# Fewer identity filler products in the attention of the first batch, with a new order table

## The chip, the core and the metric

The kernel runs on one core of a Trainium2 chip. The metric is the device time of one execution in microseconds (us); lower is better. Engines are called as in the profile: PE (TensorE, matrix products; PEld is its weight loading), DVE (VectorE), ACT (ScalarE), POOL (GpSimd) and SP (SyncE, which issues nearly all DMAs). A line L259 stands for every instruction of the first part of the program, because one helper issues them all; instructions are told apart by the names of their tiles.

## The reference

A gated linear attention, a token and channel mixer, and a gated MLP, over 4 batches of 768 positions, 8 heads of 48 channels:

```python
f = 1.0 / (1.0 + np.exp(-f_logit))
for t in range(S):
    state = f[:, :, t, :, None] * state + np.einsum('bhd,bhe->bhde', k[:, :, t], v[:, :, t])
    y[:, :, t] = np.einsum('bhd,bhde->bhe', q[:, :, t], state)
...
theta = x @ w_theta
zr, zi = x * np.cos(theta), x * np.sin(theta)
y = np.einsum('ts,bsd->btd', w_tok_r, zr) + np.einsum('ts,bsd->btd', w_tok_i, zi)
u = x + y
u + np.maximum(u @ w_ch, 0.0)
...
h = np.maximum(x @ w_in, 0.0)
u, v = (h[..., :d_ff // 2], h[..., d_ff // 2:])
v_s = np.einsum('ts,bsd->btd', w_spatial, layer_norm(v)) + b_spatial[None, :, None]
(u * v_s) @ w_out
```

(`layer_norm(v)` stands for four lines that subtract the mean and divide by the standard deviation.)

## The kernel before

**Attention of the first batch.** The positions are cut into chunks of 64, so that the recurrence becomes products. Heads go in pairs, called units u; each batch has four of them, and for the first batch each unit is done in two halves h of 384 positions (`half_att`). A half of a unit is a chain over the engines. DVE turns the gates into decays (`icp`, `cw`) and scales k and q with them (`k`, `q`). PE transposes k (`pt`, `half_k`), forms the masked scores (`psc`, `att_s`, then `sc` on DVE) and the outer products of k and v (`pw`, `half_w`); ACT copies those to `cu`, DVE scans over the chunks in `cu`, and PE multiplies q with the scanned states and the scores with v into the two output banks `px` (`half_x`). ACT copies the banks into the batch's activations `X`.

**Filler products.** Right after `half_x` takes its two output banks, it calls `warm`, which multiplies the 128x128 identity with itself four times into the first of them; the results are overwritten by the real products. In the trace they read `px<-ident`. Each fp32 product has two records, so four of them are 8 records. At the very start 16 more identity products are put into a bank `pt` (`FILL`); those stay.

**Mixer of the first batch.** `xt` are transposes of X, `pth` is theta, ACT and DVE make cosine and sine (`sn`) and multiply by X (`z`). The token weights come in 12 blocks by DMA into one of two buffers `ws` as 64-bit numbers and are turned into floats by one ACT step and three DVE steps (`tk<-ws`); the weights of theta (`ft`) and of the channel product (`wb`, `wc`) take the same way through `ws`. PE sums `acc<-tk,z`, 36 products for the first 384 output positions, then `hh` is the channel product. Batches 1 to 3 follow with split operands (three products each) while their own attention is still being computed. From 352.6 us of the span on the MLP of all batches runs (`pv`, `pu`, `pg`, `po`).

**What sets the order.** `Plan` records every instruction and its dependences; a table `LINE`, with one list of unit numbers for each queue (T for PE, V for DVE, A for ACT, G for POOL, Q for SP), gives the order in which each engine issues its units in everything before the MLP. A unit is one instruction, or on PE a group of products between two calls of `group`. An engine works strictly through its list, so an instruction that waits holds up all that stand behind it.

Of the kernel before, what the change touches and what calls it, by code (L numbers as in the profile page):

```python
# [80 lines left out]
    ],  # L81
# [18 lines left out]
    ],  # L100
# [19 lines left out]
    ],  # L120
# [1247 lines left out]
```

## Time and profile before

| | us |
|---|---|
| timed runs, median of 3 | 595.83 (594.65 to 596.77) |
| the profiled execution's own time | 598.03 |
| span of that execution | 596.3 |
| PE busy | 581.0 (97%) |
| DVE busy | 452.0 (76%) |
| ACT busy | 352.8 (59%) |
| mean granted PE clock | 0.997 |

The span runs from the first to the last instruction of the profiled execution; its own time is 1.7 us longer. Shares are means over the whole span; the attention of the first batch fills about its first 55 us.

### The profile page before, as it was taken

What the parts mean: (1) busy time and instruction counts of PE and PEld (TensorE: products, weight loads), DVE (VectorE), ACT (ScalarE), POOL (GpSimd) and SP (SyncE); (2) the same over time, 40 slices, a digit from 0 to 9 for tenths busy, and PEclk for the clock granted to TensorE, in tenths of its full rate; (3) what the DMA queues carried; (4) which work ended last, traced back from release to release, by engine and by line L of the source; (5) the groups of instructions that cost most, each with busy time, mean ns of one, the idle gap of its engine ahead of it and who ended that gap; (6) DMA issues with size and microseconds to landing.
All of it is one profiled execution on the core that took longest, in us unless ns stands there. A gap on an engine that the chain in (4) does not pass through costs nothing.

```text
span 596.3 us, 14184 instructions
## 1 busy us (share of the span) xinstructions
PE 581.0 (97%) x5750; PEld 533.3 (89%) x5750; DVE 452.0 (76%) x816; ACT 352.8 (59%) x683; POOL 29.1 (5%) x95
## 2 busy tenths in 40 slices
PE   7899998999999999999999999999999999999995
PEld 6776676877999999999999989999999999999995
DVE  6898998899887777764868587983968396839681
ACT  7798896598877888754664146623642364246421
POOL 5320110000000000000000000000000000000000
PEclk9999999999999999999999999999999999999998
DMA  7779966686978887778789999896049604940422
GB/s 240 209 240 333 281 200 250 226 287 210 304 240 307 271 311 247 256 249 282 244 282 320 338 354 299 288 373 212 1 139 373 203 1 147 371 145 0 158 89 78
DMA packets 68585, 139.44 MB, mean 234 GB/s; under 512 B 6496, under 2 KB 40800, under 8 KB 68512
## 3 DMA queue, kind: packets, MB, share of 16 engines
q1 hardware_dynamic: 68368, 138.36, 68.9%
q8 instruction: 47, 0.77, 0.6%
q14 instruction: 26, 0.21, 0.1%
q10 hardware_dynamic: 144, 0.10, 0.1%
HBM read 104.20 MB, written 31.85 MB: 228 GB/s over the span
## 4 chain that ended last, share of the span: by engine, by line
PE 91%; DMA 3%; DVE 2%; issue 1%; ACT 1%; SPq 1%; POOL 0%; DVEq 0%; ACTq 0%; POOLq 0%
PE acc L259 27%; PE pg L259 15%; PE po L259 9%; PE pu L259 8%; PE pv L259 8%; PE hh L259 6%; PE pth L259 6%; PE px L259 3%; PE psc L259 3%; PE pw L259 2%; PE pt L259 2%; DMA ws<-tok_dram 1%; SPq L259 1%; DMA k<-kd_dram 1%; DVE icp L259 1%
## 5 line engine op out<-in xcount | busy, mean ns | idle before, releaser
L259 PE MATMUL acc<-tk,z 128*128 128x384 f32 x792 | 172.4, 369 | 0.0
L259 PEld LDWEIGHTS acc<-tk,z 128*128 128x128 f32 x792 | 138.3, 189 | 15.8
L259 PE MATMUL pg<-sp,vn 128*128 128x384 f32 x504 | 88.0, 336 | 0.0
L259 PEld LDWEIGHTS pg<-sp,vn 128*128 128x128 f32 x504 | 87.4, 188 | 0.0
L259 PE MATMUL po<-wo,gt 128*128 128x384 f32 x288 | 51.3, 338 | 0.0
L259 PEld LDWEIGHTS po<-wo,gt 128*128 128x128 f32 x288 | 50.8, 188 | 0.0
L259 PE MATMUL pu<-x,wi 128*128 128x384 f32 x288 | 50.7, 335 | 0.0
L259 PEld LDWEIGHTS pu<-x,wi 128*128 128x128 f32 x288 | 50.1, 188 | 0.3
L259 PE MATMUL pv<-wi,x 128*128 128x512 f32 x216 | 49.8, 390 | 0.0
L259 PEld LDWEIGHTS pv<-wi,x 128*128 128x128 f32 x216 | 40.5, 188 | 8.2
L259 PE MATMUL hh<-uT,wc 128*128 128x384 f32 x216 | 41.9, 341 | 0.6 <-DVE uT L259 0.4
L259 ACT ACTIVATE gt<-g 128x384 fp32r<-128x384 f32 x32 | 16.7, 523 | 43.1 <-DVE g L259 42.5
L259 PEld LDWEIGHTS hh<-uT,wc 128*128 128x128 f32 x216 | 37.7, 188 | 1.6 <-DVE uT L259 0.9
L259 DVE TENSOR_TENSOR vn<-vr,vn 128x768 fp32r<-128x768 f32 x24 | 22.9, 955 | 16.1 <-ACT vn L259 15.8
L259 ACT ACTIVATE vn<-vr 128x768 fp32r<-128x768 f32 x24 | 20.2, 844 | 20.4 <-PE pg L259 17.9
L259 PE MATMUL pth<-wh,xT 128*128 128x384 f32 x108 | 31.9, 350 | 0.0
L259 DVE BATCH_NORM_STATS2 st<-vr 128x6 f32<-128x512 f32 x24 | 16.1, 687 | 19.6 <-ACT vr L259 19.6
L259 PE MATMUL px<-vc,sc 64*64 64x48 f32 x768 | 27.1, 220 | 0.2
L259 ACT ACTIVATE ws<-ws 128x768 f32<-128x768 f32 (+2 forms) x28 | 20.7, 738 | 10.4 <-DMA ws<-wo_dram 4.2
L259 ACT ACTIVATE oo<-po 128x384 f32<-128x384 f32 (+1 forms) x24 | 11.6, 482 | 24.8 <-PE po L259 23.7
L259 ACT ACTIVATE sn<-sn 128x384 f32<-128x384 f32 x48 | 24.3, 520 | 2.9 <-DVE sn L259 2.7
L259 PEld LDWEIGHTS px<-vc,sc 64*64 64x64 f32 x768 | 24.7, 140 | 0.5 <-DMA vc<-va_dram 0.3
(141 smaller groups left out, 1055.0 us busy)
## 6 DMA issues: line engine op xcount, KB each, us to landing
sp<-wpd SPq DMA_DIRECT2D x56, 576.0 KB, 5.9
tk<-tkp SPq DMA_DIRECT2D x48, 384.0 KB, 5.0
ws<-tok_dram SPq DMA_DIRECT2D x12, 768.0 KB, 5.9
tkp<-tk SPq DMA_DIRECT2D x24, 384.0 KB, 5.0
tkd<-tk SPq DMA_DIRECT2D x12, 384.0 KB, 5.7
x2d<-xt SPq DMA_DIRECT2D x24, 192.0 KB, 4.5
ws<-tkd SPq DMA_DIRECT2D x12, 384.0 KB, 4.9
xs<-x2d SPq DMA_DIRECT2D x12, 384.0 KB, 3.9
```

What stands on the lines that cost most here:

```text
L259: r = f(*a, **k)
```

## The change

`half_x` calls `warm` in the first halves alone, so that of 32 filler products in the `px` banks 16 are left. With four units fewer on PE the numbers of later units fall, and the table `LINE` is replaced by another one, which also orders the remaining units differently on all five queues. The rest of the program is the same.

```diff
@@ half_x
         ps = [self.bank("px") for _ in range(2)]
-        self.warm(ps[0])
+        if h == 0:
+            self.warm(ps[0])
         self.group()
@@ LINE, list "T"
-        45, 46, 47, 48, 49, 50, 51, 52, 53, 61, 54, 55, 56, 57, 82, 58, 59, 60, 95, 100, 91, 101, 121, 128, 132, 137, 144, 138, 148, 153, 154, 159,
...
+        45, 46, 47, 48, 61, 49, 50, 51, 52, 53, 54, 55, 82, 56, 57, 58, 59, 60, 95, 100, 91, 101, 121, 128, 132, 137, 144, 138, 148, 153, 154, 163,
...
```

How the table moves instructions is shown at three places. The first is the start of PE's queue, where identity products stand among the transposes of the first two k tiles. Before:

```order
L259 MATMUL pt<-ident 128x128 x9
L259 MATMUL pt<-ident,k_137 128x128 x3
L259 MATMUL pt<-ident 128x128 x4
L259 MATMUL pt<-ident,k_203 128x128 x3
L259 MATMUL pt<-ident 128x128 x3
L259 MATMUL pw<-vn_100,kt 64x48 x12
```

Now:

```order
L259 MATMUL pt<-ident 128x128 x4
L259 MATMUL pt<-ident,k_137 128x128 x3
L259 MATMUL pt<-ident 128x128 x7
L259 MATMUL pt<-ident,k_203 128x128 x3
L259 MATMUL pt<-ident 128x128 x5
L259 MATMUL pw<-vn_100,kt 64x48 x12
```

Of the 16 identity products five have moved from ahead of the first transposes to behind them.

The second place is PE's queue in the first half of the last unit (u = 3), where the `pw` products feed the scan that the last `px` row waits for:

```order
+L259 MATMUL pw<-vn_101,kt 64x48 x12
 L259 MATMUL psc<-qp_107,kp 64x64 x12
-L259 MATMUL pw<-vn_101,kt 64x48 x12
 L259 MATMUL px<-ident 128x128 x4
 L259 MATMUL px<-cu_480,qp_107 64x48 x2
```

The `pw` products now stand ahead of the scores; the fillers of this first half are still there.

The third place is DVE's queue in the second halves, around the first token block (`tk0_1011` before, `tk0_995` now) and the scan of unit 1 (`cu11`). Before:

```order
L259 TENSOR_SCALAR tk0_1011<-ws_1012 128x768
L259 SCALAR_TENSOR_TENSOR tk0_1011<-ws_1012,tk0_1011 128x768
L259 TENSOR_TENSOR k3_938<-k3_938,icp_98 128x768
L259 SCALAR_TENSOR_TENSOR tk0_1011<-ws_1012,tk0_1011 128x768
L259 TENSOR_TENSOR sc0_108<-psc_748,mask_91 128x384
```

Now:

```order
L259 TENSOR_SCALAR tk0_995<-ws_996 128x768
L259 SCALAR_TENSOR_TENSOR cu11_688<-cu11_688 128x336
L259 SCALAR_TENSOR_TENSOR tk0_995<-ws_996,tk0_995 128x768 x2
L259 TENSOR_TENSOR k3_922<-k3_922,icp_98 128x768
L259 TENSOR_TENSOR sc0_108<-psc_740,mask_91 128x384
```

The step on k of the next batch's first group (`k3`) used to stand between the last two steps on the block and now stands behind both, so the `ws` buffer is read out one step sooner.

## Rows read from the trace of the kernel before

**Rows 1.** The page: busy time of the engines, and granted PE clock in 40 slices.
```profile
PE 581.0 (97%) x5750; PEld 533.3 (89%) x5750; DVE 452.0 (76%) x816; ACT 352.8 (59%) x683; POOL 29.1 (5%) x95
...
PEclk9999999999999999999999999999999999999998
```

**Rows 2.** Stretches: start:end, length, busy PE, PEld, DVE, ACT, POOL (records), clock, DMA share, GB/s.
```profile
0.00:54.60 54.60, 48.09 (x908) 39.42 (x908) 46.34 (x80) 43.76 (x103) 17.49 (x60) 1.00 0.78 250
54.60:110.00 55.40, 53.60 (x881) 38.23 (x882) 50.96 (x72) 45.04 (x84) 5.81 (x12) 1.00 0.76 253
110.00:200.00 90.00, 89.80 (x1132) 78.41 (x1131) 75.98 (x105) 71.62 (x123) 2.44 (x15) 1.00 0.79 262
...
300.00:352.60 52.60, 52.18 (x298) 51.61 (x297) 39.39 (x68) 22.26 (x41) 0.10 (x1) 1.00 0.96 339
```

**Rows 3.** Timeline of PE, fillers of the second halves: start, length, what, [idle before <-releaser].
```profile
29.80 1.06 PE L259 MATMUL px<-ident 128*128 128x128 f32 x8
30.71 2.20 PE L259 MATMUL pth<-ft,xt 128*128 128x384 f32 x6
...
38.48 1.05 PE L259 MATMUL px<-ident 128*128 128x128 f32 x8
...
43.63 1.05 PE L259 MATMUL px<-ident 128*128 128x128 f32 x8
44.90 0.39 PE L259 MATMUL px<-cu,qp 64*64 64x48 f32 x8 [0.21 <-DVE cu L259]
...
50.07 1.05 PE L259 MATMUL px<-ident 128*128 128x128 f32 x8
```

**Rows 4.** Waits from 0 to 60 us: who <- for whom, total, times, longest.
```profile
PE px L259 <- DVE cu L259: 2.4, 4, 1.2
```

**Rows 5.** Timeline of DVE, 20 to 54 us.
```profile
20.42 0.86 DVE L259 TENSOR_TENSOR_SCAN cu<-cu 128x336 f32<-128x336 f32 x1 [0.37 <-ACT cu L259]
...
24.93 0.86 DVE L259 TENSOR_TENSOR_SCAN cu<-cu 128x336 f32<-128x336 f32 x1 [0.52 <-ACT cu L259]
...
29.74 0.36 DVE L259 TENSOR_SCALAR ft<-ws 128x384 uint32<-128x384 uint32 x1 [0.31 <-ACT ws L259]
30.13 1.15 DVE L259 SCALAR_TENSOR_TENSOR ft<-ws,ft 128x384 uint32<-128x384 uint32 x2
31.63 0.56 DVE L259 TENSOR_TENSOR k<-k,icp 128x384 f32<-128x384 f32 x1 [0.35 <-DMA k<-kd_dram]
...
41.32 0.96 DVE L259 SCALAR_TENSOR_TENSOR tk<-ws,tk 128x768 uint32<-128x768 uint32 x1
...
51.11 0.56 DVE L259 TENSOR_SCALAR tk<-ws 128x768 uint32<-128x768 uint32 x1 [1.26 <-ACT ws L259]
...
53.57 0.95 DVE L259 TENSOR_TENSOR z<-sn,X 128x768 f32<-128x768 f32 x1
```

**Rows 6.** Timelines of SP and ACT: the third token block's issue and its first step.
```profile
43.09 1.46 SPq L259 DMA_DIRECT2D ws<-tok_dram  x1
...
50.17 0.90 ACT L259 ACTIVATE ws<-ws 128x768 f32<-128x768 f32 x1 [1.76 <-DMA ws<-tok_dram]
```

**Rows 7.** Timelines of DVE, ACT and PE, 79 to 89 us.
```profile
79.31 0.53 DVE L259 TENSOR_TENSOR wc<-wb,wc 128x384 fp32r<-128x384 f32 x1
...
86.81 0.94 ACT L259 ACTIVATE qp<-q,live 128x768 f32<-128x768 f32 x1 [0.84 <-DVE q L259]
...
87.81 0.92 PE L259 MATMUL psc<-qp,k 64*64 64x64 f32 x24
```

**Rows 8.** Timeline of PE, the longest wait after 60 us.
```profile
98.75 1.71 PE L259 MATMUL psc<-qp,kp 64*64 64x64 f32 x47 [1.56 <-issue]
```

**Rows 9.** Timeline of PE, the first products.
```profile
2.33 3.88 PE L259 MATMUL pt<-ident 128*128 128x128 f32 x18 [2.33 <-POOL ident masks.py:199]
6.35 0.55 PE L259 MATMUL pt<-ident,k 128*128 128x128 f32 x3
6.73 1.06 PE L259 MATMUL pt<-ident 128*128 128x128 f32 x8
```

124 rows, old and new, of the table LINE are left out of this document.

## The prediction, made before the changed kernel ran

> **What bounds the kernel now.** I read the page first. PE is busy for 581.0 of 596.3 us and its clock stands at full in 39 of 40 slices [rows 1], which makes PE look like the bound everywhere. The table of stretches corrects that [rows 2]. From 110 us to the MLP, PE has next to no idle time (0.20 us of 90, then 0.42 us of the 52.6 before the MLP), so every microsecond that PE is ahead at 110 us comes off the end. But in the first 54.6 us PE is busy for only 48.09, and part of that is filler; DVE is busy there for 46.34 us. The five waits of DVE that I find from 20 us on sum to 2.8 of the 8.3 us that are left [rows 5]; most of the others lie at the start, before the first loads are there. The waits between the engines confirm the direction: PE waits for the scans of DVE, four times, 2.4 us in all [rows 4]. So until about 90 us the question for every PE step is whether DVE has its input ready, and what counts is how fast DVE gets through its list, not how much PE has to do.
>
> **The fillers.** The four groups that go take 1.06, 1.05, 1.05 and 1.05 us of PE time [rows 3]. From the start of one to the start of what follows it was 0.91 us for the first (30.71 less 29.80) and about 1.0 for the rest: 3.9 us in all. The third group shows what this is worth by itself: behind it PE still waited 0.21 us for the scan, so without the group it would wait 1.2 us and gain nothing. Nor did any filler of a second half hold DVE up: the DVE waits that I find after 29.80 us are one for a loaded k, one for a token block [rows 5] and none for PE. **Taken alone I cost the removal at 0**, covered by DVE's list; the ends are 0 and -3.9. What it does is to make PE able to follow if DVE gets faster.
>
> **DVE's list.** Up to the step that makes the third z block (at 53.57 us before [rows 5]) the new table puts the same DVE instructions ahead, in another order. So DVE can reach it sooner only by losing waits. One by one:
> - 0.52 us before the scan of unit 3's first half. Its `pw` products, which ACT has to copy first, now stand ahead of the scores, whose 24 records take 0.92 us in the like row [rows 7]; that is more than the wait. Gone: -0.52.
> - 0.37 us before the scan of unit 2's first half. In the new list the steps on the f and cw of later units stand ahead of it, so DVE arrives later than its copies: -0.37. The same steps then no longer stand behind it, so nothing is added.
> - 0.35 us for the second half of k of unit 2, and 0.31 us for the third block of theta weights. Both loads are issued sooner: in SP's list the k load goes from place 39 to 34, ahead of the first token block (768 KB) and no longer behind the gates of the next batch, and the weight load goes from 35 to 23. -0.66.
> - 1.26 us for the third token block. Its load could be issued only when DVE had read out the buffer of the first block, which ended at 41.32 + 0.96 = 42.28; the issue came at 43.09 and ACT could begin only at 50.17 [rows 5, 6]. The step on k3 (0.95 us) now stands behind that read-out instead of inside it, so of DVE's work 0.95 us more lies between release and need. The wait shrinks by that, to 0.3: -0.95.
>
> Together -2.5 us. Against it stands the start. Of the 16 identity products there, nine ran before the first transposes, at 3.88 / 9 = 0.43 us each; the next four took 1.06 us, 0.265 each [rows 9]. That ratio is what two clock levels, 1.2 and 2.4 GHz, would make, and the rise comes after the first nine, although the profile's clock column says full from the beginning. Now four run first, PE then waits for k until about 6.35, and 12 instead of 7 stand between there and `pw`. If PE is fast from there on, `pw` is 5 x 0.265 = 1.3 us later than before; if all 12 run at the slow pace, 5.2 instead of 1.9, so 3.3 us later. DVE meanwhile has the three steps of the first theta block to do, which the new list puts ahead of the first scan: 0.36 + 1.15 = 1.5 us by the same steps later on [rows 5]. What DVE then waits is between 0 and 1.8 us. I take 0.6, because the rise should come part of the way through the 12, as it came within the first 4 us before. So DVE reaches the third z block 2.5 - 0.6 = 1.9 us sooner.
>
> **From 55 to 110 us.** The tightest place is the scores of unit 6: qp is ready at 86.81 + 0.94 = 87.75 and PE starts at 87.81 [rows 7], so PE was on time within 0.06 us. Ahead of the q that feeds it the new list has the same DVE steps but one, a subtraction for the channel weights (0.53 us [rows 7]), which has moved behind: -0.53. PE has done the same 28 token products by then in both orders, and has 3.9 us of filler less, so it can follow a shift of 1.9 + 0.53 = 2.4 us. What it does with the rest is wait. Afterwards there is one long wait, 1.56 us before the scores of unit 7, for which the profile names no releaser [rows 8]. I cannot say what makes it, so I leave it as it is, at 0; the bounds are its loss and a second one like it, -1.56 and +1.56.
>
> **From 110 us on** the same products run in another order, with waits of 0.6 us before the MLP at most to win. I cost this at 0; it holds as long as PE's inputs are not later than PE, which its almost unbroken busy time speaks for. The MLP's order is the same.
>
> **Sum:** -2.5 + 0.6 - 0.53 = **-2.4 us**. The profiled execution took 598.03 us with a span of 596.3, so it would take 595.6 with a span of 593.9. The timed runs lie lower, at 595.83, and I set the forecast against them: **593.4 us**. A difference under 0.3%, 1.8 us, is about what a measurement of this kernel cannot tell from none.
>
> **Rivals.**
> - *DVE keeps its waits.* A list without one wait often gains another, and the loads are close: DMA is 0.78 busy in the first stretch [rows 2], and the first token block now waits at SP for a buffer with loads of v and k behind it. If the gains on DVE's list come back as waits for those, only the 0.53 is left: 595.3 us. For it speaks that three of the five gains hang on transfers; against it that the wait for the third block shrinks whatever the DMAs do, as long as SP issues on time.
> - *All of it arrives.* The start costs nothing, the whole 1.26 us goes, and the unexplained wait goes too: -(0.37 + 0.52 + 0.66 + 1.26 + 0.53 + 1.56) = -4.9, so 590.9 us. PE's 3.9 us and its own waits of 2.4 us [rows 4] would allow it. Against it: five things must go right.
> - *The clock falls.* This one ends slower. The fillers kept PE working while it waited for scans; without them a second half holds a wait of some 1 us at each of four places. If PE then ran the next 3.9 us at the slow pace, as it did over its first nine products [rows 9], each place would cost 3.9 x (1 - 0.265 / 0.43) = 1.5 us, 6.0 for four, against the 3.9 that PE is freed of: +2.1 us, and the gain of DVE is lost because PE comes too late for it: 597.9 us. With two falls or fewer PE still arrives before DVE and the forecast stands. The trace speaks against it: the clock stayed at 1.00 through the wait of 1.56 us [rows 2, 8], and PE keeps more work around these places than it had in the first halves.
>
> The Trainium skill speaks for the last rival (TensorE: Matmul & The Clock Gate, section "HAM oscillation — how this bites in real kernels"): a PE that idles between bursts of products is put back to half clock and begins the next burst cold. By that rule, if it bit at all four places, the time would be the 597.9 us above; by the trace, where waits of that size left the clock at full, it is 593.4.
>
> **How the numbers follow.** I give the forecast 0.50, DVE keeping its waits 0.24, all of it arriving 0.11, and the clock with whatever else the new order spoils 0.15. The forecast's own range is 592.0 to 595.2: the start between 0 and 1.8 us, and one of the two transfer gains lost. Faster by over 1.8 us means under 594.0; of the forecast's 0.50 I count 0.40 there and 0.10 above. With the second rival that is 0.51 faster. Same: 0.10 + 0.22 from the first rival + 0.02 from the last = 0.34. Slower: 0.02 from the first rival, where the unexplained wait doubles, and 0.13 from the last, 0.15. The range that holds it 8 times in 10 reaches from the second rival to the last: 590.9 to 597.9 us.
>
> **What would show it.** Right: the third z block on DVE starts near 51.7 instead of 53.57, DVE's wait before the third token block is under 0.5 us, the scans of units 2 and 3 wait for nothing, the scores of unit 6 start near 85.4, and PE's waits in the first 54.6 us add up to more than before with the span shorter nevertheless. The start is wrong if DVE waits over 1 us for the first `cu` or `psc`. The forecast as a whole is wrong if the third z block does not come sooner, if a clock below 1.00 or filler-sized products slower than 0.3 us appear between 25 and 55 us, or if PE has new waits after 110 us of over 1 us.

## The result and the profile after

The change makes the kernel slower: median 600.63 us of 6 runs (598.98 to 603.06) against 596.30 of 6 runs beside it (594.65 to 597.05), a ratio of 1.0081, 95% interval [1.0055, 1.0107]. The prediction of 593.4 (590.9 to 597.9) was wrong in sign. The profiled execution took 600.52 us with a span of 598.7, 2.4 more than before. The profiled execution of the kernel before took 598.03 us, more than any of the six runs beside the change, so the two traces side by side show 2.4 of the 4.3 us between the medians.

The page, and the table of stretches with the columns of [rows 2]:

```profile
PE 579.4 (97%) x5718; PEld 532.1 (89%) x5718; DVE 450.2 (75%) x816; ACT 353.0 (59%) x683; POOL 32.3 (5%) x95
```
```profile
0.00:54.60 54.60, 45.70 (x872) 37.79 (x873) 45.42 (x80) 43.34 (x102) 19.03 (x61) 0.97 0.77 247
54.60:110.00 55.40, 52.62 (x878) 36.74 (x877) 49.22 (x70) 45.95 (x85) 4.94 (x11) 1.00 0.76 240
110.00:200.00 90.00, 90.00 (x1135) 79.12 (x1135) 77.25 (x106) 68.78 (x122) 5.13 (x17) 1.00 0.77 266
```

Against [rows 2], PE has 32 records fewer to do, but DVE, which sets the pace, does less in each of the first two stretches (45.42 and 49.22 us instead of 46.34 and 50.96). From 110 us PE is saturated as before. And the clock of the first stretch is no longer 1.00.

**The start.** Timeline of PE, the rows that answer to [rows 9], and then the waits of DVE at the start:

```profile
1.60 2.07 PE L259 MATMUL pt<-ident 128*128 128x128 f32 x8 [1.60 <-POOL ident masks.py:199]
6.54 0.90 PE L259 MATMUL pt<-ident,k 128*128 128x128 f32 x3 [2.86 <-DVE k L259]
7.24 3.20 PE L259 MATMUL pt<-ident 128*128 128x128 f32 x14
10.22 0.85 PE L259 MATMUL pt<-ident,k 128*128 128x128 f32 x3
12.28 0.56 PE L259 MATMUL pw<-vn,kt 64*64 64x48 f32 x24
```
```profile
7.08 0.19 DVE L259 RECIPROCAL fs<-f 128x6 f32<-128x6 f32 x1 [0.60 <-ACT f L259]
7.83 0.36 DVE L259 TENSOR_SCALAR ft<-ws 128x384 uint32<-128x384 uint32 x1 [0.55 <-ACT ws L259]
14.90 0.56 DVE L259 TENSOR_TENSOR sc<-psc,mask 128x384 f32<-128x384 f32 x1 [0.36 <-PE psc L259]
```

PE waits 2.86 us for k, and the seven products behind it take 3.20 / 7 = 0.46 us each: still the slow pace. `pw` comes at 12.28 instead of 8.96 us in the timeline of the kernel before, 3.3 later. DVE waits for f1, the theta weights and the scores, 1.5 us in all.

**20 to 54 us.** Timeline of DVE, rows that answer to [rows 5]:

```profile
23.05 0.86 DVE L259 TENSOR_TENSOR_SCAN cu<-cu 128x336 f32<-128x336 f32 x1
...
27.97 0.86 DVE L259 TENSOR_TENSOR_SCAN cu<-cu 128x336 f32<-128x336 f32 x1 [1.09 <-POOL ge L259]
...
30.26 0.56 DVE L259 TENSOR_TENSOR icp<-cw,icp 128x384 f32<-128x384 f32 x1 [0.52 <-ACT ws L259]
...
35.73 0.86 DVE L259 TENSOR_TENSOR_SCAN cu<-cu 128x336 f32<-128x336 f32 x1 [0.86 <-ACT cu L259]
...
51.86 0.55 DVE L259 TENSOR_SCALAR tk<-ws 128x768 uint32<-128x768 uint32 x1
52.45 1.95 DVE L259 SCALAR_TENSOR_TENSOR tk<-ws,tk 128x768 uint32<-128x768 uint32 x2
54.32 0.95 DVE L259 TENSOR_TENSOR z<-sn,X 128x768 f32<-128x768 f32 x1
```

The waits for the scan of unit 2, for k, for the weights and for the third token block are gone, as forecast. Three others have come. The third z block starts at 54.32 instead of 53.57. Behind the 1.09 us stands ACT, in its timeline:

```profile
24.44 1.72 ACT L259 ACTIVATE f<-f 128x768 f32<-128x768 f32 x2 [1.43 <-DMA f<-fd_dram]
26.07 0.45 ACT L259 ACTIVATE X<-px 128x144 f32<-128x144 f32 x2
26.41 0.44 ACT L259 ACTIVATE cu<-kp 128x288 f32<-128x288 f32 x1
```

ACT now works on the gates f3 of the next batch ahead of the copies of units 2 and 3, and waits there for a load; the copies that PE and the scan need stand behind. (The profile puts DVE's wait down to POOL, the last of its semaphores.) The 0.86 us has SP behind it: the first token block was issued ahead of v, so PE's `pw` of the second half waits for v.

```profile
26.39 0.81 PE L259 MATMUL pw<-vn,kt 64*64 64x48 f32 x19 [0.87 <-ACT X L259]
...
27.95 1.74 PE L259 MATMUL px<-ident 128*128 128x128 f32 x8
...
34.50 0.56 PE L259 MATMUL pw<-vn,kt 64*64 64x48 f32 x24 [0.74 <-DMA vn<-vu_dram]
```

After the first of these two waits the granted clock fell to 0.50, that is 1.2 GHz, though the fillers of the first halves are all there: the four at 27.95 take 1.74 / 4 = 0.44 us each. From 32 us on the clock is 1.00 again, and it stays there after the second wait. One row per us, columns as in [rows 2]:

```profile
27.00:28.00 1.00, 1.00 (x35) 0.93 (x31) 0.03 (x1) 0.62 (x3) 0.13 (x1) 1.00 0.80 202
28.00:29.00 1.00, 1.00 (x7) 1.00 (x7) 1.00 (x2) 0.97 (x3) 0.11 (x1) 0.68 1.03 249
29.00:30.00 1.00, 1.00 (x19) 0.78 (x18) 0.74 (x2) 1.00 (x3) 0.37 (x2) 0.50 0.67 160
30.00:31.00 1.00, 1.00 (x40) 0.98 (x36) 0.70 (x2) 0.52 (x2) 0.00 (x0) 0.50 0.92 301
```

**55 to 110 us.** The waits of PE, which answer to [rows 7, 8]:

```profile
89.27 1.61 PE L259 MATMUL psc<-qp,k 64*64 64x64 f32 x48 [0.59 <-ACT qp L259]
...
97.51 1.65 PE L259 MATMUL pw<-vn,kt 64*64 64x48 f32 x46 [2.19 <-ACT X L259]
99.09 2.85 PE L259 MATMUL acc<-tk,z 128*128 128x384 f32 x8
```

The wait of 1.56 us before the scores of unit 7 is gone, but the `pw` ahead of them now wait 2.19 us.

### The profile page after: what moved, and what is told of

It reads as the page before. It is cut to its first block, busy times and chain, and to the rows that moved or that the text cites. A ratio compares the mean times of both kernels' runs of the same rounds, so it can differ in the third digit from the quotient of the medians.

```text
span 598.7 us, 14114 instructions
## 1 busy us (share of the span) xinstructions
PE 579.4 (97%) x5718; PEld 532.1 (89%) x5718; DVE 450.2 (75%) x816; ACT 353.0 (59%) x683; POOL 32.3 (5%) x95
## 4 chain that ended last, share of the span: by engine, by line
PE 89%; DMA 4%; DVE 3%; issue 1%; ACT 1%; SPq 1%; POOL 0%; DVEq 0%; ACTq 0%
PE acc L259 25%; PE pg L259 15%; PE po L259 8%; PE pu L259 8%; PE pv L259 8%; PE hh L259 6%; PE pth L259 6%; PE px L259 3%; PE pt L259 3%; PE psc L259 3%; PE pw L259 2%; DMA f<-fd_dram 1%; DMA vn<-vu_dram 1%; DMA ws<-wc_dram 1%; DMA ws<-tok_dram 1%
```

## The experiments

Each run stands beside runs of the kernel before that were made with it. The ratio is not the quotient of the two medians.

| run | median | before beside it | ratio, 95% interval |
|---|---|---|---|
| fillers alone | 595.76 | 596.84 | 0.9990 [0.9975, 1.0005] |
| order alone | 609.36 | 596.84 | 1.0206 [1.0168, 1.0244] |
| no px fillers | 598.56 | 597.08 | 1.0033 [1.0020, 1.0045] |
| order of before to 54 us | 599.15 | 596.74 | 1.0045 [1.0027, 1.0063] |
| changed order to 54 us | 598.33 | 596.74 | 1.0031 [1.0005, 1.0058] |
| changed order to 20 us | 598.30 | 597.08 | 1.0035 [1.0015, 1.0054] |

**Fillers alone and order alone.** The units of the four groups (228, 265, 281, 296) are taken out of PE's list and the others renumbered; or they are put back into the list of the change.

```diff
-            self.warm(ps[0])
+            if h == 0:
+                self.warm(ps[0])
...
-        300, 302, 228, 304, 229,
+        296, 298, 300, 228,
```

> The order of before, with the four filler groups of the second halves left out and nothing moved. Before: 596.3 us; the change: 600.6. The start theory (the change loses because PE's identity products at the start were moved behind the first transposes, so that `pw` comes 3.3 us later) expects no difference from before: 595.5 to 597, and `pw` at 9.0 us of the span as before. The clock theory (without fillers PE is put back to half clock) expects half-clock stretches between 30 and 52 us and 598 to 600. The order theory (the rest of the table loses) expects 595 to 597.

> The table of the change with the four filler groups put back at the places they had before. The start theory expects a time at or above that of the change, 600 to 604, since the 3.3 us lost at the start stay and PE has 3.9 us more to do. The clock theory expects 596 to 598. The order theory expects 600 to 603.

Without the fillers and with nothing moved, 0.9990: no loss. The order with the fillers loses 2.06%. So the order loses, and the fillers hide nothing of it: in the new order they cost 1.0206 less 1.0081, 1.25% or 7.5 us, more than their 3.9 us of PE. In that profile the clock of 54.6 to 110 us is 0.94, in that of the change 1.00, and PE has waits of 1.02, 1.45 and 1.52 us between 185 and 270 us, where the change has one of 0.75.

**Early or late.** Two hybrids without the fillers: every list follows one order as far as it was by 54 us, then takes what is left in the other. The first hybrid begins with the order of before, the second with the changed one. In PE's list of the first, for instance:

```diff
@@ LINE, list "T"
-        293, 409, 431, 446, 458, 340, 342, 386, 432, 344,
+        293, 431, 386, 340, 342, 409, 446, 458, 432, 344,
```

> The second-half fillers left out; every queue in the order of before as far as it was by 54 us, from there the changed order for all that is left. The run with the fillers left out of the order of before took 595.76 us (596.84 for the kernel before beside it), the change 600.6. Early theory (the changed table loses in the first 54 us, where DVE, ACT and SP wait in new places, and only carries that loss on): 595 to 597. Late theory (it loses after 54 us, by a wait like that of 2.19 us for ACT's X at 97.5 us, and by the clock): 599 to 601. If both halves carry part: about 598.

> The complement: the changed order as far as each queue was by 54 us in the changed kernel, from there the order of before, second-half fillers left out. Early theory: 599 to 601. Late theory: 595.5 to 597. Both: about 598.

Both lose. Against the fillers alone, the late part costs 1.0045 less 0.9990, 3.3 us, the early part 2.4 us; together 5.7 us. The change stands 1.0081 less 0.9990, 5.4 us, above the fillers alone, so the two parts make up its loss, within the intervals.

**The late part.** In the first hybrid PE's wait is the only one over 0.2 us from 52 to 110 us, and what follows is at half clock:

```profile
94.43 1.68 PE L256 MATMUL pw<-vn,kt 64*64 64x48 f32 x46 [2.33 <-ACT X L256]
96.04 5.33 PE L256 MATMUL acc<-tk,z 128*128 128x384 f32 x8
```
```profile
92.00:94.00 2.00, 0.10 (x1) 0.00 (x0) 0.52 (x2) 0.80 (x2) 0.11 (x1) 1.00 0.98 240
94.00:96.00 2.00, 1.57 (x46) 1.52 (x46) 1.82 (x3) 1.09 (x4) 0.00 (x0) 0.56 1.01 377
96.00:98.00 2.00, 2.00 (x6) 1.17 (x4) 1.33 (x3) 1.78 (x5) 0.00 (x0) 0.50 0.58 220
```

ACT's list in that trace, where the copies X that the `pw` need stand behind a step on a token block:

```profile
93.20 0.88 ACT L256 ACTIVATE ws<-ws 128x768 f32<-128x768 f32 x1 [2.19 <-DMA ws<-tok_dram]
93.98 0.69 ACT L256 ACTIVATE X<-px 128x288 f32<-128x288 f32 x2
```

The same edit on the change and on this hybrid puts two groups of token products (545 and 558) ahead of the `pw` of unit 7 (563). The kernel before has one of the two there, 545; the change had moved it behind.

```diff
@@ LINE, list "T"
-        557, 554, 559, 563, 545, 558, 568,
+        557, 554, 559, 545, 558, 563, 568,
```

> The change with one edit on PE: ahead of the `pw` products of unit 7, which wait 2.19 us for ACT's copies X at 97.5 us, go the two groups of token products (`acc`, 1.4 us each) that the change put behind them; before had one of them there. If that wait and the half-speed stretch that can follow it are the late loss, the wait shrinks to 0 to 0.3 us and the time falls by 2 to 3.5 us, to 597 to 598.5. If the waits only move on, 600 to 601.

> The same edit on the hybrid with the order of before up to 54 us (599.15), whose PE waited 2.33 us at 94.4 and then ran at half clock for 6.8 us. If this one place is the whole late loss: 595.5 to 597, and no half clock between 90 and 105 us. If the later order loses elsewhere too: 598 to 599.

Measured: 598.89 against 596.37, 1.0040 [1.0022, 1.0059], and 596.37 against 596.37, 0.9990 [0.9971, 1.0008]: 2.4 us less in the change (1.0081 less 1.0040), 3.3 us less in the hybrid. In the hybrid the eight records of `acc` take 2.85 us instead of 5.33, and of the wait 0.27 us is left:

```profile
92.72 2.85 PE L256 MATMUL acc<-tk,z 128*128 128x384 f32 x8
95.50 1.65 PE L256 MATMUL pw<-vn,kt 64*64 64x48 f32 x48
...
98.24 0.91 PE L256 MATMUL psc<-qp,kp 64*64 64x64 f32 x23 [0.27 <-issue]
```

That one place is the whole late loss, 1.0045 to 0.9990, though the edit puts one group more ahead of the `pw` than the kernel before has there. PE had nothing left to do while ACT's copies X, behind a step that waits 2.19 us for a token block (2.11 in the change), were late.

In the order of before the same copies stand behind the same step. Whether they make its wait of 1.56 us [rows 8]:

```diff
@@ LINE, list "A"
-        562, 517, 527, 560, 561, 506,
+        562, 517, 560, 561, 527, 506,
```

> The order of before without the second-half fillers (595.76), with one edit on ACT: the two copies X of unit 6, which stand behind a step on a token block that waits 1.7 us for its load, go ahead of that step. If the wait of 0.6 to 1.6 us before the scores of unit 7, for which the profile names no releaser, comes from these late copies, it goes, and the time falls to 594.5 to 595.5. If it has another cause, 595.5 to 596.5 and the wait stays.

595.65 against 596.37, 0.9993 [0.9974, 1.0013], and the wait stays:

```profile
97.53 0.73 PE L256 MATMUL psc<-qp,kp 64*64 64x64 f32 x17 [1.50 <-issue]
```

So they don't; what does is open.

**The early part, its middle.** Three edits on the waits between 20 and 35 us: the gate steps f3 on ACT back (on the change), the load of the first token block on SP back (on the second hybrid), and both with ACT's step on that block (on the second hybrid).

```diff
@@ LINE, list "A"
-        149, 150, 326, 327, 155, 156,
+        149, 150, 155, 156,
...
+        297, 299, 326, 327, 241,
@@ LINE, list "Q"
-        195, 367, 216, 253, 191, 233, 217, 252, 192,
+        195, 216, 253, 191, 233, 217, 252, 367, 192,
```

> The change with one pair of ACT's steps moved: those on the gates f3 of the next batch, which ACT reaches at 23 us and then waits 1.43 us for their load, go back behind the copies `xt`, where before had them; nothing else. If that wait makes the late X and the late scan of unit 3 (DVE waits 1.09 us for it) and sets the lag after, the third z block comes about 1.0 to 1.5 us sooner than in the change (54.3) and the time falls by 1 to 1.5, to 599.2 to 599.7. If the lag is set elsewhere (start, loads of v, the later order), 600 to 601.

> The hybrid with the changed order up to 54 us (598.33), with one edit on SP: the load of the first token block (768 KB, 1.5 us to issue), which the change put ahead of the loads of v for the second halves, goes behind them. If that load makes PE wait 1.59 us for vn at 33.5 and DVE 1.22 us for the scan behind it, both waits fall under 0.4 us, the third z block comes 0.8 to 1.3 us sooner, and the time is 597 to 597.7. If the early loss is set by the start alone, 598 to 598.6.

> The hybrid with the changed order up to 54 us (598.33), with three moves at once, each back to about its place in before: ACT's steps on the gates f3 behind the copies `xt`, SP's load of the first token block behind the loads of v, ACT's step on that block behind the copies for the second scan. If these three places are the early loss, no wait over 0.6 us on PE between 20 and 50 us and 595.8 to 597. If the start carries it: 598 to 599.

Measured 1.0109 [1.0091, 1.0128], 1.0060 [1.0036, 1.0084] and 1.0028 [1.0001, 1.0055]. None gains. Each takes away the wait that it was aimed at and meets the next. With the gate steps back the scan no longer waits, but PE then waits longer for the following `pw`; with the token load back PE no longer waits for v, and ACT waits for the block instead (timelines of PE and of ACT):

```profile
32.94 0.56 PE L256 MATMUL pw<-vn,kt 64*64 64x48 f32 x24 [1.86 <-ACT cw L256]
```
```profile
37.37 0.89 ACT L256 ACTIVATE ws<-ws 128x768 f32<-128x768 f32 x1 [3.18 <-DMA ws<-tok_dram]
```

**The early part, its start.** The changed order to 20 us alone, then that of before:

```diff
@@ LINE, list "T"
-        144, 138, 148, 153, 154, 163, 159, 168,
+        144, 138, 148, 153, 154, 159, 163, 168,
```

> Second-half fillers left out; the changed order only as far as each queue was by 20 us, from there the order of before. Changed order up to 54 us: 598.33; order of before throughout: 595.76. If the start carries the early loss: 597.5 to 599. If the waits between 20 and 54 us carry it: 595.5 to 596.7.

598.30 against 597.08, 1.0035: as much as the changed order to 54 us (1.0031). The third z block starts 2.93 us later than with the fillers alone (54.74 against 51.81), and the last long row of `hh` before the MLP 2.72 us later (348.52 against 345.80), so here the lag of the start goes nearly whole to the end. DVE's z block in this run, then in the one with the fillers alone:

```profile
54.74 0.95 DVE L256 TENSOR_TENSOR z<-sn,X 128x768 f32<-128x768 f32 x1
```
```profile
51.81 0.95 DVE L256 TENSOR_TENSOR z<-sn,X 128x768 f32<-128x768 f32 x1
```

Its DVE before that:

```profile
6.76 0.19 DVE L256 RECIPROCAL fs<-f 128x6 f32<-128x6 f32 x1 [0.36 <-ACT f L256]
7.61 0.36 DVE L256 TENSOR_SCALAR ft<-ws 128x384 uint32<-128x384 uint32 x1 [0.66 <-ACT ws L256]
...
15.06 0.56 DVE L256 TENSOR_TENSOR sc<-psc,mask 128x384 f32<-128x384 f32 x1 [0.55 <-PE psc L256]
...
23.28 0.86 DVE L256 TENSOR_TENSOR_SCAN cu<-cu 128x336 f32<-128x336 f32 x1 [1.82 <-ACT cu L256]
```

3.4 us of waits. The longest, 1.82 us, lies behind the cut at 20 us. The whole changed order has no wait there (23.05, above), since it does steps on f and cw first, and the fillers alone have 0.35 us; so the cut may add to the 2.7 us. The changed order to 54 us, with no cut there, gives 2.4 us for start and middle together. Parts of the start: the identity products in the old places in the change, in the new places in the kernel before, and the first theta blocks (loads, ACT's and DVE's steps) back in the run above.

```diff
@@ LINE, list "T"
-        45, 46, 47, 48, 61, 49, 50, 51, 52, 53, 54, 55, 82, 56,
+        45, 46, 47, 48, 49, 50, 51, 52, 53, 61, 54, 55, 56, 57, 82, 58,
@@ LINE, list "V"
-        18, 8, 20, 24, 70, 32, 72, 25, 76, 26, 33, 27, 77, 34, 109,
+        18, 8, 20, 24, 70, 72, 25, 76, 26, 27, 77, 109,
...
```

> The change, with the 16 identity products at the start put back as before (9, 4 and 3 instead of 4, 7 and 5), nothing else. The start theory expects the slow products to end near 6 us instead of 11, `pw` near 9 to 9.5 us instead of 12.3, no half-clock stretch near 30 us, and 594 to 597 us. The clock theory expects a half-clock stretch still and about 600. The order theory expects 599 to 600.5.

> Before, with only the identity products at the start moved as the change has them (4, 7 and 5 instead of 9, 4 and 3). The start theory expects `pw` near 12 us and 598.5 to 600.5 us. The clock theory (only the fillers in the second halves matter) and the order theory (the rest of the table) expect 596 to 597.

> The run with the changed order only up to 20 us (598.3), with the first blocks of theta weights back at about their places in before on SP, ACT and DVE (load, one ACT step, three DVE steps); the identity products and the other loads at the start stay as changed. If the weight block ahead of the loads of f, k and v and its three DVE steps ahead of the first scan are what the start costs: the first scan at 12.1 to 12.6 us instead of 13.6, and 596 to 597. If it is the identity products or the other loads: 597.8 to 598.8.

Measured 1.0067 [1.0045, 1.0088], 1.0012 [0.9990, 1.0033] and 1.0023 [1.0008, 1.0037]. The start theory, that the identity products make the whole loss, falls with the first two. A part of it is not excluded. With them back in the change, `pw` comes at 11.10 us and not near 9, since PE still waits 0.64 us for k and the products behind stay slow. With only them moved in the kernel before, the first scan comes 1.70 us later (13.55 against 11.85) and the third z block no later (53.27 against 53.57): the waits of 0.52, 0.31 and 0.35 us [rows 5] and most of the 1.26 are gone there and took up the delay. The theta blocks alone are not all of it either: the scan of the first unit comes 0.4 us sooner, and DVE waits for f1 (0.59 us) and f2 (0.82 us) instead. The start costs as a whole; how it divides is open.

Three runs tell less. The first 12.5 us of all lists as before, the rest changed, cuts the order at a bad place: DVE's steps on the theta block come to stand ahead of the first `sc` while their load is late, and PE waits 4.94 us there; 605.22 against 596.74, 1.0149 [1.0129, 1.0170].

> The change with the first 12.5 us of every queue ordered as before (identity products, loads, and the steps on gates and theta weights), the rest as in the change. If the start as a whole (loads and DVE's list with it, not the identity products alone) carries the loss, `pw` at 9 us, the third z block at 52 to 53 and 597 to 598.5. If not, DVE waits for the same things later, and 599.5 to 601.

And the moves at once: the late and the middle ones in the change, 599.24 against 597.08, 1.0057 [1.0037, 1.0078], and the late one with the theta blocks, 600.15 against 597.13, 1.0048 [1.0031, 1.0066]. Neither gets back to before: the identity products and the order of the loads at the start are still the changed ones in both.

> The change (600.6) with all four moves: the three of the run before it and the two groups of token products ahead of the `pw` of unit 7. If these places are the whole loss: 596 to 597.5. If the start carries the early part: 597.5 to 599.

> The change (600.6) with the weight blocks moved back as in the run beside it and the two groups of token products ahead of the `pw` of unit 7; all other places of its order stay. If start and late wait are the whole loss and the rest of the new order keeps its gains (DVE's wait of 1.26 us for the third token block), 594.5 to 596.5. If the waits for f3 and v between 20 and 35 us count once the start is repaired: 597 to 598.5.

**The clock.** The order of before without any filler in a `px` bank:

```diff
-        if h == 0:
-            self.warm(ps[0])
```

> The order of before with no filler products in any px bank (those at the very start stay). The fillers of the first halves take another 3.9 us of PE. If waits of DVE set the pace there, 595 to 596.5, as with the second-half fillers alone left out. If PE's clock needs them, half-clock stretches between 10 and 30 us, and 597 to 600.

598.56 against 597.08, 1.0033 [1.0020, 1.0045], slower than with the first halves' fillers although PE has another 4 us less to do. DVE now waits 0.82 and 1.20 us for PE's scores at 24.4 and 30.6 us, and its third z block starts at 53.33 instead of 51.81. Its PE, and its clock:

```profile
21.55 0.35 PE L256 MATMUL px<-cu,qp 64*64 64x48 f32 x2 [1.67 <-DVE cu L256]
```
```profile
20.00:22.00 2.00, 0.45 (x17) 0.48 (x20) 1.57 (x3) 1.97 (x6) 0.53 (x1) 0.85 0.49 98
22.00:24.00 2.00, 2.00 (x65) 2.00 (x60) 1.55 (x4) 1.02 (x4) 1.14 (x4) 0.50 0.85 260
...
28.00:30.00 2.00, 1.99 (x23) 1.49 (x23) 1.41 (x3) 1.58 (x6) 0.85 (x3) 0.56 0.89 252
```

## Why the prediction was wrong

**The fillers at 0** was right, in the order of before: 0.9990, and the clock there stayed at 1.00 from 20 to 54.6 us through new waits of 0.58 and 1.20 us in the second halves. But the sign that the prediction named for DVE's new list, a third z block near 51.7, came there with nothing moved: 51.81, and 51.66 to 52.04 in the three other traces with this order to 54 us. DVE's wait for the third token block is 0.72 us at most in these four, against 1.26 in the one trace of the kernel before from which the prediction took its gain. In the changed order the 0 was wrong by its cover: there PE came late, and the four groups with what followed were worth 7.5 us.

**DVE's list** was half right. Of the five waits four went, with 0.37 + 0.66 + 1.26 = 2.3 us. The fifth, 0.52 us before the scan of unit 3, became 1.09: the step argued from `pw` on PE alone, and ACT's list, which holds the copies in between, had a wait for f3's load put ahead of them. The loads of the token block and of v, which the first rival named, brought 0.86 us, ACT's weight step 0.52. What is left is small: the changed order to 54 us costs about as much as to 20 us (1.0031 and 1.0035).

**The start, +0.6 with at most 1.8**, is the first term that failed. With the cut at 20 us it measured 2.7 us (1.0035 less 0.9990), with the cut at 54 us and all that the middle adds 2.4. The upper price of `pw`, 3.3 us later, is what came, since the products behind the wait of 2.86 us stayed slow. But the term covered it with DVE's three theta steps as if DVE were only waiting for PE. DVE waited for its loads as well, 0.60 us for f1 and 0.55 for the theta weights, and those steps stood in the chain to the first scan. The sign that the prediction gave for this term, over 1 us of waiting for the first `cu` or `psc`, did not show (0.36 us for `psc`): it looked for PE, and DVE's larger waits there were for loads. Moving the theta steps back brought the first scan 0.4 us, so how much each of these weighs is open.

**55 to 110 us** is the second. The -0.53 did not show: the scores of unit 6 start 1.46 us later (89.27 against 87.81), after waits of DVE of 1.03 us for PE's `acc` and 0.98 us for a weight load:

```profile
61.94 0.56 DVE L259 TENSOR_SCALAR tk<-ws 128x768 uint32<-128x768 uint32 x1 [1.03 <-PE acc L259]
```
```profile
74.78 0.37 DVE L259 TENSOR_SCALAR wb<-ws 128x384 uint32<-128x384 uint32 x1 [0.98 <-ACT ws L259]
```

And "I leave it as it is, at 0" for the long wait left out that a group of token products had moved from ahead of the `pw` to behind them. That place measured 2.4 us in the change and 3.3 in the hybrid, above the bound of +1.56, because the price of a wait on PE can include a stretch at half clock behind it.

**From 110 us on at 0** held within 0.8 us in the profiled execution: one new wait of 0.75 us at 259 us.

**The rivals.** The clock rival had the right sign and the wrong place: the clock fell behind no removed filler, but after the wait of 0.87 us in a first half and, in the hybrid, near 95 us. By the rule of the Trainium skill (TensorE: Matmul & The Clock Gate, section "HAM oscillation — how this bites in real kernels") a PE that idles between bursts of products begins the next one at the lower clock. The hybrid's trace agrees, where a wait of 2.33 us was followed by products at half clock, and so does the 0.87 us in the change; in the run with the fillers alone, waits up to 1.20 us were not so followed. In the profiled execution of the change, the 2.19 us at 97.5 us was not followed by a fall either. Of the six traces with this order at this place it is the only one: in the other five (order alone, identity products back, first hybrid, gate steps back, first 12.5 us as before) the eight records of `acc` behind waits of 2.06 to 2.45 us take 3.79 to 5.33 us instead of 2.85. So the length of the wait alone does not decide, and the trace of the change may show less of the late loss than its other runs have, which spread over 4 us with mean clocks from 0.991 to 0.995.

No version beat the kernel before by more than the noise; the nearest are the fillers alone and the first hybrid with the token products ahead, both 0.9990, and the fillers alone with ACT's copies moved, 0.9993.

## What to carry to other kernels

When an order is changed, follow each step that a critical engine waits for through the lists of all engines it passes, and look for an in-order step ahead of it that waits for a load. A pacing engine's delay in the first 20 us can go to the end nearly whole (2.72 of 2.93 us here) where no wait behind it can take it up, and cost nothing where there are such waits, so the start needs its own count. Where PE has work that doesn't depend on a late copy, it belongs ahead of what does; taking work away elsewhere doesn't pay for that wait.

## What was not expected of the hardware

The granted clock column reads 1.00 for the first microseconds of every profile, while the products there take 0.43 to 0.46 us each, and 0.265 later; the durations tell it, not the column. With the wait of 2.86 us in between, the slow pace lasted past 10 us instead of 6. And 2.6 us of lost time came from removing 16 identity products whose results are overwritten (1.0033 less 0.9990, twelve runs each): behind waits of 1.67 and 1.68 us PE ran at half clock, as it did not with the products there.
